# Attention and a SwiGLU block on one core: splitting 448 keys as three chunks of 128 and a rest of 64 that four heads share

## The chip, the cores and the metric

The kernel runs on one core of a Trainium2 chip. The metric is the device time in microseconds (us). Before the change it is 453.3 us, the median of three runs (453.28 to 453.46). The profiled execution has a span of 451.7 us from its first to its last instruction.

A core has TensorE (matrix products; in the profile PE, and PEld for the load of its stationary operand), ScalarE (ACT), VectorE (DVE), GpSimd (POOL) and SyncE (SP), which here only issues transfers. TensorE writes into PSUM, which has eight banks of 512 float32 columns by 128 partitions. ScalarE and VectorE move results from there to SBUF.

## The reference, cut to what matters

Eight sequences of 448 tokens, twelve heads of 64: 96 softmax attentions. Their outputs, joined to 768 features a token, go through a gated feed-forward block.

```python
batch, n_heads, seq, head_dim = (8, 12, 448, 64)
scores = scale * np.matmul(q, k.transpose(0, 1, 3, 2))
attn = np.exp(scores - np.max(scores, axis=-1, keepdims=True))
attn = attn / (np.sum(attn, axis=-1, keepdims=True) + 1e-09)
x = np.matmul(attn, v)                     # then (3584 tokens, 768)

n_tokens, d_model, d_ff = (3584, 768, 1536)
g = x @ w_gate
silu = g * (1.0 / (1.0 + np.exp(-g)))
out = silu * (x @ w_val) @ w_out
```

## The kernel before

Two heads of one sequence form a pair; there are 48. For a pair, `q` and `k` are turned so that the 64 features lie on partitions: head 0 on partitions 0 to 63, head 1 on 64 to 127. Pairs 0 to 10 are turned by TensorE, later ones by DMA transposes. The scores come with the keys on partitions, in four chunks of 112 keys. Both heads' matmuls contract 64 rows, each in its own half of the array, and one exponential on ScalarE takes both.

```python
P = 112; NC = S // P          # 4 chunks of 112 keys
NPE = 11; FIRST = 6; XPE = 12; NE = 4; NX = 6

def qk(pr, c):
    t = qkT[pr]
    s = ps_s.tile([128, 2, 512], FP32, tag="s")          # two banks, three such buffers
    for hx in range(2):
        nc.tensor.matmul(
            s[:, hx, 0:S],
            lhsT=t[ts(hx, 64), c * P : c * P + 128],
            rhs=t[ts(hx, 64), ds(S + (1 - hx) * D, S)],
            start=True, stop=True,
        )
    e = Es[pr % NE][:, ds(c * EB, 16)].rearrange("p (h b) x -> p h (b x)", h=2)
    nc.scalar.activation(e[:, :, 0:S], s[0:P, :, 0:S], AF.Exp, scale=sm_scale)
```

The product with the values has the queries on partitions. `vo` holds a column of ones after the 64 values, so that column 64 of the accumulator is the softmax sum. The 2 x 448 queries of a pair are seven blocks of 128, the last of which is half of each head; they share one bank. Four chunks times eight matmuls are 32 a pair. VectorE then divides.

```python
def pv_chunk(pr, c):
    if c == 0:
        accs[pr] = ps_f.tile([128, 512], FP32, tag="f", name="acc")   # one bank, two buffers
    ...
    for j in range(3):
        for hx in range(2):
            nc.tensor.matmul(a7[:, 2 * j + hx], lhsT=e[...128 queries], rhs=vo[:, hx, c, 0 : D + 1], ...)
    for hx in range(2):
        nc.tensor.matmul(a7[:, 6], lhsT=e[...64 queries and zeros], rhs=vo[:, hx, c, 0 : D + 1], ...)
    if c < NC - 1:
        return
    nc.vector.reciprocal(r[:, 0:7], a7[:, :, D])
    nc.vector.tensor_tensor(xt[:, 0:n], a7[:, 0:n, 0:D], r[...broadcast], ALU.mult)
    # ... pairs from XPE on: two small multiplications more, for the seventh block
```

`turn_x` turns the result so that features lie on partitions (X): pairs 0 to 11 by TensorE against an identity (with `turn_rests` for the seventh blocks of six pairs together), later ones by DMA transposes. X feeds the feed-forward block, which is cut into eight blocks of 384 or 512 tokens. A step `fv` makes 128 hidden features of a block: six matmuls for the gate (`gp`), six for the value (`vp`), a tanh on ScalarE (`sg`), two operations on VectorE (`t`, `hts`). A step `o` makes 128 tokens by 384 output features with twelve matmuls (`op`), which ScalarE evicts and SyncE stores.

```python
gp = ps_s.tile(...)[:, 0]            # or one of the two small banks, after a visit without a product
group("g", gp)                       # 6 matmuls of 128 x n
nc.scalar.activation(sg[:, 0:n], gp[:, 0:n], AF.Tanh, scale=0.5)
vp = ps_f.tile([128, 512], FP32, tag="f", name="vp")
group("v", vp)
...
last = last_block and ch == n // 128 - 1      # the last 128 tokens: stored in three parts
```

The program first does the attention of pairs 0 to 5 (one whole sequence), then goes through *visits*. A visit makes the next two or three score chunks, the product of a pair whose exponentials are ready, and the steps `fv` and `o` of an earlier sequence. After the last pair only feed-forward steps remain.

Of the kernel before, what the change touches and what calls it, by code (L numbers as in the profile page):

```python
# [19 lines left out]
NPE = 11  # L20
# [3 lines left out]
WIDE = 8  # L24
XPE = 12
NE = 4
NX = 6
NV = 5
VS = 9
EB = 15  # L30
# [3 lines left out]
def kernel(  # L34
# [24 lines left out]
    MQ = S - D  # L59
# [13 lines left out]
    load_table("exp_and_others")  # L73

# [7 lines left out]
    ps_f = ctx.enter_context(tc.tile_pool(name="ps_f", bufs=2, space=PSUM))  # L82

    Es = [consts.tile([P, NC * EB + 1, D], FP16, name=f"E{i}") for i in range(NE)]
    Xts = [consts.tile([128, 7, D], FP16, name=f"xt{i}") for i in range(NX)]
    Xrs = [consts.tile([D, 128], FP16, name=f"xr{i}") for i in range(3)]
    Vts = [consts.tile([P, 2, NC, D + 2], FP16, name=f"vo{i}") for i in range(NV)]
    vraw = consts.tile([P, VS, 2, NC, D], FP16, name="vraw")
# [11 lines left out]
    wo = [consts.tile([128, NFB, OH], FP16, name=f"wo{i}") for i in range(2)]  # L100
# [5 lines left out]
    def dummy(n):  # L106
        wp = ps_f.tile([128, 512], FP32, tag="f", name="wp")
        for _ in range(n):
            nc.tensor.matmul(wp[:], lhsT=warm[:, 0:128], rhs=warm[:], start=True, stop=True)  # L109

    def load_qk32(pr):
        rq = raws.tile([P, 2, NC, D], FP32, tag="rq", bufs=RB)
        rk = raws.tile([P, 2, NC, D], FP32, tag="rk", bufs=RB)
        for dst, src in ((rq, q), (rk, k)):
            nc.sync.dma_start(dst[:], src[0, 2 * pr : 2 * pr + 2].rearrange("h (p c) d -> p h (c d)", c=NC))
        raw[pr] = (rq[:], rk[:])
# [3 lines left out]
    def load_qk16(pr, n=2):  # L120
        h0 = 2 * (pr % 2) if pr >= 14 else 0
        if h0 == 0:
            q16 = raws.tile([P, 4, NC, D], FP16, tag="rq", bufs=RB, name="q16")
            k16 = raws.tile([P, 4, NC, D], FP16, tag="rk", bufs=RB, name="k16")
            pairbuf[:] = [q16, k16]
        q16, k16 = pairbuf
        for dst, src in ((q16, q), (k16, k)):
            flat = src.rearrange("b h s d -> (b h) s d")[2 * pr : 2 * pr + 2 * n]
            nc.gpsimd.dma_start(dst[:, ds(h0, 2 * n)], flat.rearrange("h (p c) d -> p h (c d)", c=NC))  # L129
        for i in range(n):  # L130
            h = h0 + 2 * i
            raw[pr + i] = (q16[:, h : h + 2], k16[:, h : h + 2])

    def load_v(pr, n=1):
        b, h = divmod(2 * pr, H)
        nc.gpsimd.dma_start(  # L136
            vraw[:, ds(pr % VS, n)].rearrange("p r h c d -> p (r h) (c d)"),
            v[b, h : h + 2 * n].rearrange("h (p c) d -> p h (c d)", c=NC),
        )
# [4 lines left out]
    def load_w(kind, i):  # L144
        if kind == "o":
            src = moe_w_out[:, ts(i, OH)].rearrange("(f p) m -> p f m", p=128)
            dst = wo[i]
        else:
            src = (moe_w_gate if kind == "g" else moe_w_val)[:, ts(i, DF // 4)].rearrange(
                "(t a p) m -> t p a m", p=128, t=2  # L150
            )
            for t in range(2):
                nc.gpsimd.dma_start(wgv[kind, i][:, ts(t, NCB // 2), :], src[t])
            return
        nc.gpsimd.dma_start(dst[:], src)

    def prep(pr):
        rq, rk = raw[pr]
        if pr == 0 or pr >= NPE:
            qk16 = attp.tile([P, 2, NC, 2, D], FP16, tag="qk16", bufs=3)  # L160
            for t, src in enumerate((rq, rk)):
                dst = qk16[:, 1 - t].rearrange("p c h d -> p h c d")
                if pr == 0:
                    nc.vector.tensor_copy(dst[:, 0], src[:, 0])
                    nc.scalar.activation(dst[:, 1], src[:, 1], AF.Copy)
                else:
                    nc.gpsimd.tensor_copy(dst, src)  # L167
        qkT[pr] = attp.tile([128, 2 * S + D], FP16, tag="qkT", name="qkT", bufs=5)
        if pr >= NPE:
            nc.sync.dma_start_transpose(  # L170
                qkT[pr][:, 0 : 2 * S].rearrange("p (c q) -> p c q", q=P),
                qk16[:].rearrange("p t c h d -> p (t c h d)"),
            )
            nc.sync.dma_start_transpose(
                qkT[pr][:, 2 * S :].rearrange("p (c q) -> p c q", c=1),
                qk16[0:D, 1, 0].rearrange("p h d -> p (h d)"),
            )
            return None

        def turn0():  # L180
            for t in range(2):
                tp = ps_s.tile([128, 2, 512], FP32, tag="s", name="tp")
                for c in range(NC):
                    for hx in range(2):
                        nc.tensor.matmul(
                            tp[ts(hx, 64), c // 2, ds(c % 2 * P, P)],
                            lhsT=qk16[:, 1 - t, c, hx],
                            rhs=ident[0:P, 0:P],
                            start=True,
                            stop=True,  # L190
                        )
                dst = qkT[pr][:, ts(1 - t, S)].rearrange("p (a x) -> p a x", a=2)
                nc.vector.tensor_copy(dst[:, 0], tp[:, 0, 0 : 2 * P])
                nc.scalar.activation(dst[:, 1], tp[:, 1, 0 : 2 * P], AF.Copy)
                if t == 0:
                    tq = tp
            nc.vector.tensor_copy(qkT[pr][:, 2 * S :], tq[:, 0, 0:D])

        def turn():
            if pr < FIRST + 2:  # L200
                tp = ps_s.tile([128, 2, 1024], FP16, tag="s", name="tp")[:, 0]
            else:
                tp = ps_f.tile([128, 1024], FP16, tag="f", name="tp")
            for i in range(2 * NC + 1):
                t, c = (1 - i // NC, i % NC) if i < 2 * NC else (0, 0)
                for hx in range(2):
                    src = raw[pr][t][:, hx, c, :]
                    nc.tensor.transpose(tp[ts(hx, 64), ts(i, P)], src, ident[0:P, 0:P])  # L208
            nc.vector.tensor_copy(qkT[pr][:], tp[:, 0 : 2 * S + D])  # L209

        return turn if pr else turn0

    def qk(pr, c):
        t = qkT[pr]
        s = ps_s.tile([128, 2, 512], FP32, tag="s")
        for hx in range(2):
            nc.tensor.matmul(  # L217
                s[:, hx, 0:S],
                lhsT=t[ts(hx, 64), c * P : c * P + 128],
                rhs=t[ts(hx, 64), ds(S + (1 - hx) * D, S)],  # L220
                start=True,
                stop=True,
            )
        e = Es[pr % NE][:, ds(c * EB, 16)].rearrange("p (h b) x -> p h (b x)", h=2)
        nc.scalar.activation(e[:, :, 0:S], s[0:P, :, 0:S], AF.Exp, scale=sm_scale)  # L225

    def qk_half(pr, half, between=None):
        for c in (2 * half, 2 * half + 1):
            qk(pr, c)
            if between and c % 2 == 0:  # L230
                between()
# [3 lines left out]
    def pv_chunk(pr, c):  # L235
        if c == 0:
            accs[pr] = ps_f.tile([128, 512], FP32, tag="f", name="acc")
        e = Es[pr % NE]
        vo = Vts[pr % NV]
        a7 = accs[pr][:, 0 : 7 * (D + 1)].rearrange("p (s d) -> p s d", s=7)  # L240
        for j in range(3):
            for hx in range(2):
                nc.tensor.matmul(  # L243
                    a7[:, 2 * j + hx],
                    lhsT=e[:, ds(c * EB + 9 * hx + 2 * j, 2)].rearrange("p b x -> p (b x)"),
                    rhs=vo[:, hx, c, 0 : D + 1],
                    start=c + j + hx == 0,
                    stop=False,
                )
        for hx in range(2):  # L250
            nc.tensor.matmul(  # L251
                a7[:, 6],
                lhsT=e[:, ds(c * EB + 6 + hx, 2)].rearrange("p b x -> p (b x)"),
                rhs=vo[:, hx, c, 0 : D + 1],
                start=False,
                stop=c == NC - 1 and hx == 1,
            )
        if c < NC - 1:
            return
        r = attp.tile([128, 8], FP32, tag="R", bufs=2, name="R")  # L260
        xt = Xts[pr % NX]
        nc.vector.reciprocal(r[:, 0:7], a7[:, :, D])  # L262
        n = 7 if pr < XPE else 6
        nc.vector.tensor_tensor(  # L264
            xt[:, 0:n],
            a7[:, 0:n, 0:D],
            r[:, 0:n].unsqueeze(2).to_broadcast([128, n, D]),
            ALU.mult,
# [373 lines left out]
```

The softmax here doesn't subtract the row's maximum and nothing guards it: scores larger than these inputs give would overflow.

## Time and profile before

| What | Value |
|---|---|
| Device time, median of 3 | 453.3 us |
| Span of the profile | 451.7 us |
| Exponentials, ScalarE | 192, of 919 ns |
| Score matmuls, 64 rows by 448 columns | 384 |
| Product matmuls, 112 rows by 65 columns | 1536 |
| Gate, value and output matmuls | 576, 576, 684 |
| Turns of q and k by DMA, turns of X by DMA | 37 pairs, 36 pairs |
| Loads of q, k and v that GpSimd issues, one issue | 660 to 666 ns |

How to read it: a row of the profile names a source line, an engine and an operation, then out<-in by tile names, partitions by elements, and the count. `s` are scores, `E` exponentials, `acc` a product's accumulator, `xt` the divided result, `tp` a turn in PSUM. The duration of a matmul in the profile includes its latency and overlaps with the next one; the distance between starts says how often the array takes one. The profile's share of busy time is a mean over stages that have different limits.

### The profile page before, as it was taken

Reading aid. Unit: us, or ns where it says so; the run is one execution under the profiler, and the core shown is the slowest. Engines: PE = TensorE matmul, PEld = TensorE weight load, DVE = VectorE, ACT = ScalarE, POOL = GpSimd, SP = SyncE. Lnnn points to the kernel's source line nnn. Section 1 sums busy time; section 2 is a strip of 40 time slices with the busy share of each in tenths; the row PEclk is TensorE's granted clock in tenths of the full one; section 3 lists DMA queues with packets and bytes.
Section 4 is the critical chain, followed back from the end, with each engine's and each line's share of the span. In section 5 each row is a group of like instructions: output and inputs, shape, how many; then the busy total and the mean of one; then the engine's idle time right before and its main releaser. Section 6 shows DMA issues by size and latency. Waiting matters only on the chain.

```text
span 451.7 us, 9871 instructions
## 1 busy us (share of the span) xinstructions
PE 441.9 (98%) x4024; PEld 247.0 (55%) x4024; DVE 201.6 (45%) x447; ACT 238.8 (53%) x350; POOL 141.8 (31%) x228
## 2 busy tenths in 40 slices
PE   8999999999999999999999999999999999999995
PEld 3655565545455556454555656545455666544563
DVE  3666562456654434455443534353453544055300
ACT  6965666566746465554554546644555462222221
POOL 8755715927642225252313405330100000000000
PEclk9999999999999999999999999999999999999999
DMA  9999999999969379874749758772503112200033
GB/s 142 173 200 201 196 172 174 180 209 119 145 93 133 46 129 124 132 120 71 126 74 120 98 78 143 118 105 68 101 20 68 46 46 57 70 2 0 17 100 95
DMA packets 105101, 48.71 MB, mean 108 GB/s; under 512 B 59744, under 2 KB 101600, under 8 KB 105056
## 3 DMA queue, kind: packets, MB, share of 16 engines
q0 software_dynamic: 43392, 23.37, 41.2%
q1 hardware_dynamic: 61664, 24.71, 28.9%
q8 instruction: 31, 0.51, 0.5%
q14 instruction: 14, 0.11, 0.1%
HBM read 47.19 MB, written 11.01 MB: 129 GB/s over the span
## 4 chain that ended last, share of the span: by engine, by line
PE 93%; DVE 3%; ACT 2%; issue 1%; DVEq 0%; ACTq 0%
PE op L371 24%; PE gp L326 23%; PE vp L326 23%; PE s L217 9%; PE acc L243 9%; PE acc L251 2%; ACT E L225 2%; PE tp L208 1%; PE wp L109 1%; DVE t L345 1%; ACT sg L341 1%; DVE qkT L209 0%; DVE xt L264 0%; PE acc L291 0%; DVE hts L348 0%
## 5 line engine op out<-in xcount | busy, mean ns | idle before, releaser
L225 ACT ACTIVATE E<-s 112x896 f16<-112x896 f32 x192 | 162.1, 919 | 27.5 <-PE s L217 27.4
L326 PE MATMUL gp<-X,wg 128*128 128x384 f16 (+1 forms) x576 | 124.7, 352 | 0.0
L326 PE MATMUL vp<-X,wv 128*128 128x384 f16 (+1 forms) x576 | 124.6, 352 | 0.0
L371 PE MATMUL op<-wo,hts 128*128 128x384 f16 (+1 forms) x684 | 116.1, 323 | 0.0
L345 DVE SCALAR_TENSOR_TENSOR t<-sg,gp 128x384 f32<-128x384 f32 (+1 forms) x96 | 59.7, 621 | 121.8 <-ACT sg L341 121.8
L341 ACT ACTIVATE sg<-gp 128x384 f32<-128x384 f32 (+1 forms) x96 | 52.5, 547 | 84.8 <-PE gp L326 83.6
L371 PEld LDWEIGHTS <-hts 128*128 128x128 f16 x684 | 65.5, 98 | 45.9 <-issue 3.9
L326 PEld LDWEIGHTS <-wv 128*128 128x128 f16 x576 | 56.3, 98 | 52.6
L326 PEld LDWEIGHTS <-wg 128*128 128x128 f16 x576 | 53.1, 97 | 45.6 <-issue 1.1
L378 ACT ACTIVATE osb<-op 128x384 f32<-128x384 f32 (+1 forms) x57 | 27.8, 487 | 92.5 <-PE op L371 92.5
L167 POOL COPY qk<-q 112x512 f16<-112x512 f16 x37 | 22.9, 619 | 144.5 <-DMA qkT<-qk 143.1
L348 DVE SCALAR_TENSOR_TENSOR hts<-t,vp 128x384 f16<-128x384 f32 (+1 forms) x96 | 59.6, 621 | 10.0
L243 PEld LDWEIGHTS <-E 112*128 112x128 f16 x1152 | 46.7, 97 | 18.2 <-issue 17.5
L243 PE MATMUL acc<-vo,E 112*128 112x65 f16 x1152 | 53.0, 193 | 1.3 <-DVE vo L142 0.7
L217 PE MATMUL s<-qkT 64*128 64x448 f16 x384 | 50.6, 355 | 0.2
L251 PE MATMUL acc<-vo,E 112*128 112x65 f16 x384 | 42.9, 193 | 0.0
L262 DVE RECIPROCAL R<-acc 128x7 f32<-128x7 f32 x48 | 9.8, 205 | 70.6 <-PE acc L251 70.5
L129 POOL DMA_DIRECT2D k<-in_k_dram x44 | 29.0, 660 | 9.5 <-DMA wo<-in_moe_w_out_dram 7.8
L129 POOL DMA_DIRECT2D q<-in_q_dram x44 | 29.3, 666 | 5.2 <-PE s L217 2.5
L136 POOL DMA_DIRECT2D vraw<-in_v_dram x42 | 28.0, 666 | 8.4 <-DVE vo L142 7.2
L217 PEld LDWEIGHTS <-qkT 64*128 64x128 f16 x384 | 14.5, 94 | 25.8 <-issue 18.6
L264 DVE TENSOR_TENSOR xt<-acc,R 128x384 f16<-128x384 f32 (+1 forms) x48 | 27.6, 574 | 1.7
(41 smaller groups left out, 148.2 us busy)
## 6 DMA issues: line engine op xcount, KB each, us to landing
q<-in_q_dram POOLq DMA_DIRECT2D x41, 112.0 KB, 4.0
k<-in_k_dram POOLq DMA_DIRECT2D x41, 112.0 KB, 4.6
vraw<-in_v_dram POOLq DMA_DIRECT2D x39, 112.0 KB, 4.6
wg<-in_moe_w_gate_dram POOLq DMA_DIRECT2D x8, 288.0 KB, 10.1
wv<-in_moe_w_val_dram POOLq DMA_DIRECT2D x8, 288.0 KB, 10.2
wo<-in_moe_w_out_dram POOLq DMA_DIRECT2D x2, 1152.0 KB, 22.0
out_dram<-osb SPq DMA_DIRECT2D x8, 288.0 KB, 3.0
out_dram<-osb SPq DMA_DIRECT2D x8, 240.0 KB, 3.1
```

The lines of the kernel that those rows point to most:

```text
L129: nc.gpsimd.dma_start(dst[:, ds(h0, 2 * n)], flat.rearrange("h (p c) d -> p h (c d)", c=NC))
L136: nc.gpsimd.dma_start(vraw[:, ds(pr % VS, n)].rearrange("p r h c d -> p (r h) (c d)"), v[b, h : h + 2 * n].rearrange("h (p c) d -> p h (c ...
L217: nc.tensor.matmul(s[:, hx, 0:S], lhsT=t[ts(hx, 64), c * P : c * P + 128], rhs=t[ts(hx, 64), ds(S + (1 - hx) * D, S)], start=True, stop=True,)
L225: nc.scalar.activation(e[:, :, 0:S], s[0:P, :, 0:S], AF.Exp, scale=sm_scale)
L243: nc.tensor.matmul(a7[:, 2 * j + hx], lhsT=e[:, ds(c * EB + 9 * hx + 2 * j, 2)].rearrange("p b x -> p (b x)"), rhs=vo[:, hx, c, 0 : D + 1] ...
L251: nc.tensor.matmul(a7[:, 6], lhsT=e[:, ds(c * EB + 6 + hx, 2)].rearrange("p b x -> p (b x)"), rhs=vo[:, hx, c, 0 : D + 1], start=False, st ...
L326: nc.tensor.matmul(dst[:, 0:n], lhsT=wslice(kind, fb, cb), rhs=X[kk][:, cb, ds(c0, n)], start=(cb == 0), stop=(cb == NCB - 1),)
L341: nc.scalar.activation(sg[:, 0:n], gp[:, 0:n], AF.Tanh, scale=0.5)
L345: nc.vector.scalar_tensor_tensor(t1[:, 0:n], sg[:, 0:n], 1.0, gp[:, 0:n], ALU.add, ALU.mult)
L348: nc.vector.scalar_tensor_tensor(hts[:, fb, 0:n], t1[:, 0:n], 0.5 * HS, vp[:, 0:n], ALU.mult, ALU.mult)
L371: nc.tensor.matmul(op[:, 0:w], lhsT=hts[:, fb, ts(ch, 128)], rhs=wo[oh][:, fb, ds(m0 - oh * OH, w)], start=(fb == 0), stop=(fb == NFB - 1),)
L378: nc.scalar.activation(osb[:, ds(m0, w)], op[:, 0:w], AF.Copy, scale=1.0 / HS)
```

## The change

The keys of a head are split otherwise: three chunks of 128 and a rest of 64. Head `hx` of pair `pr` has its rest at the front of its keys if `hx == pr % 2` ("low"), and at the back if not. So the rests of the four heads of two neighbouring pairs fill a whole 128-partition score tile of two banks: four 64x64 matmuls, one in each quadrant of the array, and one exponential. This is for filling all 128 partitions in the exponentials and in the main score and product matmuls. K and V are loaded so that keys lie 64 to a partition group, with the two halves of the partitions starting three key columns apart.

Further parts:
- TensorE turns q and k of pairs 0 to 13 (before 0 to 10), and X of pairs 0 to 17 (before 0 to 11). The rest of 64 queries is turned with the pair; `turn_rests` goes.
- A pair's product has an accumulator for each head: in the first six pairs and the last two one two-bank tile, between them the two small banks. In a visit, the X of the pair before is turned between the products of the two heads, into a score buffer.
- The six first pairs go by a fixed string of steps (`START`: s scores, t turn, v copy of values, p product piece, x turn of X, d idle matmul).
- The number of `fv` and `o` steps of each visit is planned ahead. The output steps of the first block run later, and `w_out` is loaded later, in four pieces.
- The first pair's q is loaded from ScalarE's queue and its k from SyncE's.
- In the output step a variable `n` is set to 112 inside the loop that stores rows.

```diff
-NPE = 11
+NPE = 14
-XPE = 12
+XPE = 18
-NX = 6
+NX = 3
+NR = 3
...
     def qk(pr, c):
-        t = qkT[pr]
         s = ps_s.tile([128, 2, 512], FP32, tag="s")
-        for hx in range(2):
-            nc.tensor.matmul(
-                s[:, hx, 0:S],
-                lhsT=t[ts(hx, 64), c * P : c * P + 128],
...
+        if c < KR:
+            t = qkT[pr]
             for hx in range(2):
                 nc.tensor.matmul(
+                    s[:, hx, 0:S],
+                    lhsT=t[ts(hx, 64), ts(c + low(pr, hx), 128)],
+                    rhs=t[ts(hx, 64), ds(NC * 128, S)],
...
+        else:
+            for hx in range(2):
+                for p in (pr, pr + 1):
+                    lo = low(p, hx)
+                    t = qkT[p]
+                    nc.tensor.matmul(
+                        s[ts(1 - lo, 64), hx, 0:S],
+                        lhsT=t[ts(hx, 64), ds(0 if lo else KR * 128 + 64, 64)],
+                        rhs=t[ts(hx, 64), ds(NC * 128, S)],
...
+            e = Ers[pr // 2 % NR][:]
...
+    def pv_mm(pr, hx, c, j):
+        lo = low(pr, hx)
...
+        if c < KR:
+            rows, e, col = slice(0, 128), Es[pr % NE][:, c], c + lo
+        else:
+            rows, e, col = (slice(0, 64), Ers[pr // 2 % NR], 0) if lo else (slice(64, 128), Ers[pr // 2 % NR], KR)
+        nc.tensor.matmul(
+            accs[pr][0][hx][:, ts(j, D + 1)],
+            lhsT=e[rows, ds(hx * S + j * 128, 128)],
+            rhs=Vts[pr % NV][rows, hx, col, 0 : D + 1],
...
+    def pv_open(pr):
+            if wide(pr):
+                acc = psum["a"].tile([128, 2, 512], FP32, tag="a", name="acc") if pr < FIRST else ps_s.tile(...)
+            else:
+                accs[pr] = ([fbank(), fbank()], [0, 0])
...
+    def pv(pr, mid):
+        for hx in range(2):
+            for c in range(KR):
+                pv_piece(pr, c, (hx,))
+            if hx == 0:
+                mid()                      # run_turns: turn_x of the pair before
+        pv_close(pr)
...
         if pr < XPE:
-            tp = accs[pr] if pr < FIRST else ps_f.tile([128, 512], FP32, tag="f", name="xtp")
-            for j in range(3):
+            tp = ps_s.tile([128, 2, 512], FP32, tag="s", name="xtp")[:, 0]
+            for j in range(KR + 1):
+                n = min(128, S - j * 128)
...
     def ffn2_steps(kk, c0, n, hts, first, last_block):
...
             last = last_block and ch == n // 128 - 1
...
-                    c, p0 = divmod((j + D) % S, P)
-                    m = min(P - p0, l0 + 128 - l, (MQ if j < MQ else S) - j)
+                    n = S // NC
+                    c, p0 = divmod(j, n)
+                    m = min(n - p0, l0 + 128 - l)
```

In a visit the shared rest's scores come first, then the chunks of 128, then the product's rest pieces, then its main pieces:

```diff
+                for pr, c in sorted(chunks, key=lambda x: -(x[1] == RU)):
+                    qk(pr, c)
+                for _, p0 in todo:
+                    pv_piece(p0, RU)
```

## The prediction

> **What bounds the kernel now.** I read the engine table of the page first, then the chain that ended last, then the stretches, and last the timeline of one cycle of the steady part.
>
> ```profile
> PE 441.9 (98%) x4024; PEld 247.0 (55%) x4024; DVE 201.6 (45%) x447; ACT 238.8 (53%) x350; POOL 141.8 (31%) x228
> ...
> PE 93%; DVE 3%; ACT 2%; issue 1%; DVEq 0%; ACTq 0%
> ```
>
> TensorE is on the chain for 93% of the span, so a microsecond taken from TensorE's own work is nearly a microsecond of time, and work taken from ScalarE (53%) or the DMA queues is not. The 98% alone would not prove that, since a pipelined matmul's duration holds its latency. So I looked where TensorE really waits (the stretches; columns: length, then busy time of PE, PEld, DVE, ACT and POOL):
>
> ```profile
> 6.00:30.00 24.00, 22.13 (x394) 14.23 (x394) 13.48 (x31) 22.10 (x27) 17.08 (x25) 1.00 1.33 178
> 30.00:86.00 56.00, 54.74 (x621) 33.68 (x620) 28.22 (x60) 34.42 (x49) 31.75 (x48) 1.00 1.34 182
> 86.00:386.00 300.00, 299.77 (x2657) 164.84 (x2654) 139.70 (x317) 164.90 (x243) 88.11 (x144) 1.00 0.65 101
> ```
>
> There are three regimes. Up to 29.8 us (the first `gp`) six pairs of heads go through attention before any feed-forward block can run; there TensorE and ScalarE are both over 90% busy. From 30 to 86 TensorE loses about 1.3 us. From 86 to 386 it loses nothing. After 386 there is only feed-forward, which the change hardly touches. So the costs of single instructions must come from the timeline (start, length, instructions):
>
> ```profile
> 207.21 2.11 PE L371 MATMUL op<-wo,hts 128*128 128x384 f16 x12
> 209.25 0.74 PE L217 MATMUL s<-qkT 64*128 64x448 f16 x6
> 209.93 0.36 PE L243 MATMUL acc<-vo,E 112*128 112x65 f16 x6
> ...
> 210.90 1.46 PE L326 MATMUL gp<-X,wg 128*128 128x512 f16 x6
> 212.20 1.46 PE L326 MATMUL vp<-X,wv 128*128 128x512 f16 x6
> 213.59 0.74 PE L217 MATMUL s<-qkT 64*128 64x448 f16 x6
> 214.26 1.96 PE L371 MATMUL op<-wo,hts 128*128 128x384 f16 x11
> ```
>
> Read start to start. Six 512-column matmuls take 212.20 - 210.90 = 1.30 us, 0.216 each, or 0.42 ns a column; 448 columns are then 0.19 us and 384 are 0.162. A product takes 210.90 - 209.93 = 0.97 us for its 32 matmuls: 0.030 each. Six score matmuls would be 1.13 us one by one, but the next group starts 0.68 us later: two run at once (three streams of 0.19), and about 0.1 us is left over. On the way in, six `vp` from 212.20 should end at 213.50, and the scores start at 213.59: again 0.1. So each change between 64-row scores and 128-row work costs 0.1 us.
>
> **What the Trainium skill says.** "TensorEngine Tiling (Array Packing)", Key Properties: a change of tiling mode drains the array, and different tiles run in parallel. Both agree with the trace (0.1 us; two scores in one stream). Its Available Configurations give four tiles in 64x64 mode; no trace here has four at once yet. "PSUM — Partial Sum Buffer", PSUM bank collisions, says that two row tiles may not write one bank at the same time, which fits the new code's separate bank for each head. "Perfetto Trace Analysis", Identifying the Most-Contended Engine, warns that matmul busy share is a bad measure, which is why I work from starts.
>
> **The change part by part, on TensorE.** Counts are from the order of the built instructions.
>
> 1. *Scores.* A head has 448 keys. Before, they were four chunks of 112; a pair cost four streams, 48 x 4 = 192 in all. Now each head has three chunks of 128 and a rest of 64, and the rests of two pairs (four heads) fill one 128-row score tile as four 64x64 matmuls. Streams: 48 x 3 + 24 = 168, if the four run together. 24 x 0.19 = **-4.5 us**. The exponentials fall from 192 to 168.
> 2. *Products.* Still 32 matmuls of 65 columns a pair, but 8 have only 64 keys, in opposite halves of the array for the two heads. If they run two by two, a pair of them should take about 0.033 us (64 columns in the trace's rest turns: 24 matmuls, 0.8 us busy with the latency of the last, hence some 0.03 per two). Before 32 x 0.0303 = 0.97; now 24 x 0.0303 + 4 x 0.033 = 0.86. 48 x 0.11 = **-5.3 us**.
> 3. *Turns of q and k.* TensorE turns pairs 0 to 13 now, not 0 to 10: three more. One turn was 18 matmuls in about 0.45 us (7.00 to 7.56 with a drain, in the first turn); the new one has 16 of 64 columns (0.24) and 8 of 112 (0.19). 14 x 0.43 against 11 x 0.43: **+1.4 us**, rounded up for the larger first two.
> 4. *Turns of X.* Eighteen pairs instead of twelve: 54 matmuls of 128 columns and 18 of 64, against 36 and 24 narrow ones. At 0.056 and 0.03: 3.5 against 2.4, **+1.1 us**.
> 5. *Mode changes.* Counting along TensorE's order, before has 172 and after 187. There are fewer visits (three score units each, fewer units), but a visit with a shared rest goes 128 -> 64x64 -> 64x128 -> 128, and a turn goes through 64x64 and 128x64. 15 x 0.1 = **+1.5 us**.
> 6. One idle matmul less: **-0.2 us**. Feed-forward is the same 774,144 columns; the last output piece is no longer split.
>
> Sum: -4.5 - 5.3 + 1.4 + 1.1 + 1.5 - 0.2 = **-6.0 us**.
>
> **Off TensorE.** *The start.* Its TensorE part falls by about 1.5 us (inside the sum), and ScalarE must do 21 exponentials, not 24, before the sixth pair's product: at 0.84 us each (6 in 5.04 us in the timeline) 2.5 us less. Against it, the accumulator of a pair is now a two-bank tile with one buffer, so each pair waits for the division of the one before; reciprocal and division took 0.2 and 0.63 us. I let the start gain just what TensorE's sum says. *The steady part.* A product now holds both small banks, so the last `vp` or `op` must be evicted before it. The scores and drains between take about 0.75 us; an `hts` of 512 columns takes 0.69 and an `osb` 0.49. It fits, barely. From 30 to 60 us VectorE has per visit about 3.9 us (two divisions, X, qkT, vo, t, hts, sized from their rows) against some 4.5 us of TensorE: tight, so I expect waits of about 2 us in all, as now. *The end.* In the new output step a loop variable `n` is overwritten with 112, so the test for the last piece is never true. The last 128 rows are then stored whole: an eviction of 0.49 instead of 0.33, then a 336 KB store behind a 48 KB one. The last split stores landed 2.0 us after issue, a large quiet one about 3.6, and the old end had four issues of 0.6 in a row, which go. Net **+0.8 us**.
>
> 453.3 - 6.0 + 0.8 = **448.1 us**.
>
> **Rivals.** *A: the small tiles don't run together.* For: four at once isn't seen in any trace here. Against: two by two is. Without it in the scores, +24 x 0.19 = 4.5 (452.6); without it in the products, +5.3 (453.4); with neither, 458. *B: PSUM becomes the wait.* Products now need both small banks, and each X turn takes a score buffer. For: the tight margins above. Against: VectorE is at 45%. At 0.1 us for some 50 visits, +5: 453. *C: the start was ScalarE's.* For: 22.10 busy of 24. Then the start falls by 2.5 or more, with q and k of the first pair on two queues: about 446.5. *D: GpSimd's issues.* Value and key loads come in two halves each: 224 loads instead of 148, and 76 more at 0.66 us are 50 us on an engine that is 31% busy. On the other side six turns of X and three of q and k leave the DMA transposes. I expect nothing of it after 90 us; in the first 90 us a late weight could cost 1 or 2 us.
>
> **Range and chances.** A and B push up by up to 5 us, C down by 2 and a perfect start by 3. I take 448.1 with 444.0 to 452.5. Faster by over 2% needs under 444.2, for which the start and every bank must work out: 0.11. Slower by over 2% (462.4) needs A twice and B: 0.02. Within 2%: 0.87.
>
> **What would show it.** Right: three score streams and a four-tile one of about 0.2 us start to start; 8 rest products in about 0.13 us; first `gp` at about 28 us; no TensorE waits over 0.3 us after 100 us; the last store landing about 1 us later after the last matmul than before. Wrong: rest products at 0.24 us a pair, `er` scores taking 0.38 or more (A); TensorE waiting for `f` evictions (B); TensorE waiting for a DMA (D); first `gp` after 30 us (the single accumulator).

## The result, and the profile after

The changed kernel takes 455.5 us, median of four runs (454.74 to 455.66), beside 453.38 us (453.28 to 453.64) for the kernel before on the same chip. The ratio is 1.0042, 95% interval 1.0025 to 1.006: 0.4% slower, and 3 us above the predicted range.

The engine table of the changed kernel's page, and the shares of its chain that ended last:

```profile
PE 441.6 (97%) x4163; PEld 248.8 (55%) x4163; DVE 206.0 (45%) x464; ACT 220.1 (48%) x325; POOL 178.8 (39%) x298
...
PE 79%; DMA 12%; POOL 3%; DVE 2%; ACT 2%; issue 1%; SPq 0%; DVEq 0%; POOLq 0%
```

TensorE's busy time is what it was (441.6 against 441.9), although it has less to do; the reason is that a matmul's duration contains its latency, so this figure can't show a saving. ScalarE lost 19 us, as 24 exponentials fell away. The new thing is the chain: 12% of it is now DMA, where there was none. The stretches (columns as in the prediction):

```profile
6.00:30.00 24.00, 22.71 (x451) 14.96 (x450) 14.92 (x32) 20.48 (x25) 17.56 (x27) 1.00 1.29 181
30.00:86.00 56.00, 52.60 (x701) 31.90 (x700) 35.96 (x84) 34.19 (x46) 36.01 (x57) 1.00 1.30 180
86.00:386.00 300.00, 298.62 (x2645) 166.92 (x2644) 134.63 (x307) 147.76 (x223) 120.42 (x204) 1.00 0.72 100
```

TensorE now stands still for 3.4 us between 30 and 86 (before 1.3) and 1.4 us after that (before 0.2). That is still too little, for the same reason: the latency of the last matmul hides the first part of every wait. So I went through the starts of all matmuls, and counted as a wait what a start comes later than the one before plus that one's own pace (0.19 us for 448 columns, 0.03 for 65, and so on) and the drain, where there is one. Between the first `gp` and 390 us this gives **9.4 us of waits** (5.85 before 90 us, 3.55 after), against 2.3 us in the kernel before. The span divides like this:

| Part of the span | Before, us | After, us | Difference |
|---|---|---|---|
| To the first `gp` | 29.79 | 28.07 | -1.7 |
| First `gp` to the end of the last matmul's columns | 416.6 | 420.6 | +4.0 |
| of which waits of TensorE | 2.3 | 9.4 | +7.1 |
| of which the rest, TensorE's own work | 414.3 | 411.2 | -3.1 |
| From there to the end | 5.34 | 5.16 | -0.2 |

The work did fall, and more waiting than that came in. Whose waits they are, in the changed kernel's list of waits, from 30 to 90 us (who waited <- for whom: us in total, times, longest):

```profile
PE tp L246 <- ACT er L277: 1.1, 2, 0.6
PE s L256 <- DMA qkT<-qk: 0.7, 1, 0.7
PE s L256 <- DVE X L371: 0.7, 1, 0.7
PE f L291 <- DVE hts L410: 0.5, 3, 0.2
```

and from 90 to 390 us:

```profile
PE f L291 <- DVE hts L410: 1.0, 5, 0.2
```

By my count from the starts, the last kind is the largest of all: 13 times a product's rest pieces wait for `hts` to give back the small bank, 0.18 to 0.36 us each and 3.9 us in all; the list shows 8 of them with what is left of each after the latency. The others are the score buffers (about 2.9 us until an exponential ends and a turn or a gate may write, 0.87 more for X's copy out of one), evictions of the output step (0.56) and one DMA transpose (0.88). The timeline of one visit of the changed kernel shows the bank wait (start, length, instructions):

```profile
212.68 1.46 PE L388 MATMUL f<-X,wv 128*128 128x512 f16 x6
214.07 0.74 PE L256 MATMUL s<-qkT 64*128 64x448 f16 x6
214.64 0.19 PE L291 MATMUL f<-vo,er 64*128 64x65 f16 x1
215.04 0.28 PE L291 MATMUL f<-vo,er 64*128 64x65 f16 x7 [0.20 <-DVE hts L410]
215.25 0.91 PE L291 MATMUL f<-vo,E 128*128 128x65 f16 x24
```

and VectorE in the same stretch:

```profile
214.30 0.69 DVE L410 SCALAR_TENSOR_TENSOR hts<-t,f 128x512 f16<-128x512 f32 x1
```

The value group ends at about 213.98 (212.68 and six times 0.216), the three pairs of scores take until 214.64. The first rest piece goes into one small bank; the second head's piece needs the other, from which VectorE is still multiplying (`hts` runs from 214.30 to 214.99), and starts at 215.04. The prediction knew this wait and called it a fit.

The same view has the good news. Another visit of the changed kernel, in which the bank was free:

```profile
238.33 0.38 PE L269 MATMUL s<-qkT 64*64 64x448 f16 x4
238.65 0.55 PE L256 MATMUL s<-qkT 64*128 64x448 f16 x4
239.03 0.28 PE L291 MATMUL f<-vo,er 64*128 64x65 f16 x8
239.25 0.91 PE L291 MATMUL f<-vo,E 128*128 128x65 f16 x24
239.99 0.81 PE L388 MATMUL gp<-X,wg 128*128 128x384 f16 x4
```

Four 64x64 scores take 238.65 - 238.33 = 0.32 us: one stream of 0.19 and a drain of some 0.12, so all four run together (their starts lie within 0.01 us). Eight rest pieces and the drain behind them take 0.22 us. The whole product takes 0.96 us from 239.03 to 239.99 with that drain inside it, against 0.97 before, where the drain lay ahead of it.

The chain leaves TensorE for the DMA at one place, 70.42 us; what it holds before that is almost all loads and GpSimd's issues of them. The chain of the changed kernel between 55 and 71 us (start, us, what):

```profile
55.93 0.75 POOL wo L173
...
57.59 0.78 POOL wo L173
58.36 1.18 POOL qk L195 x2
...
60.44 9.84 DMA qkT<-qk
70.42 0.37 PE s L256 x2
```

GpSimd issues two pieces of `w_out`, then copies pair 14's q and k for the transposes, of which the second takes 9.84 us to land, at 70.28; pair 14's first scores wait for it. Here that costs 0.88 us. But it is a second limit right behind the first: had TensorE come to 69 us earlier, it would have waited longer.

**Theories to test.** T1: the small banks (a product needs both at once) hold the steady part. T2: the DMA transpose of pair 14, behind `w_out` in a full queue, takes back whatever is gained before 70 us. Rival R1: the small tiles cost more than thought. Rival R2: moving X between the heads and turning pairs 12 to 17 on TensorE is what costs.

### The profile page after: what moved, and what is told of

Read it like the earlier page. It is cut to its first block, busy times and chain, and to the rows that moved or that the text cites. A ratio compares the mean times of both kernels' runs of the same rounds, so it can differ in the third digit from the quotient of the medians.

```text
span 453.9 us, 10198 instructions
## 1 busy us (share of the span) xinstructions
PE 441.6 (97%) x4163; PEld 248.8 (55%) x4163; DVE 206.0 (45%) x464; ACT 220.1 (48%) x325; POOL 178.8 (39%) x298
## 4 chain that ended last, share of the span: by engine, by line
PE 79%; DMA 12%; POOL 3%; DVE 2%; ACT 2%; issue 1%; SPq 0%; DVEq 0%; POOLq 0%
PE f L433 24%; PE f L388 22%; PE gp L388 20%; PE f L291 7%; DMA wv<-in_moe_w_val_dram 4%; PE s L256 4%; DMA wg<-in_moe_w_gate_dram 4%; DMA qkT<-qk 2%; DMA k<-in_k_dram 1%; PE s L269 1%; DVE hts L410 1%; DVE t L407 1%; ACT sg L403 1%; POOL vraw L124 1%; POOL q L154 0%
## 5 line engine op out<-in xcount | busy, mean ns | idle before, releaser
L277 ACT ACTIVATE E<-s 128x896 f16<-128x896 f32 x144 | 123.0, 922 | 12.9 <-PE s L256 12.6
L388 PE MATMUL f<-X,wv 128*128 128x384 f16 (+1 forms) x576 | 124.7, 353 | 0.0
L433 PE MATMUL f<-wo,hts 128*128 128x384 f16 x672 | 115.5, 326 | 0.0
L388 PE MATMUL gp<-X,wg 128*128 128x512 f16 (+1 forms) x522 | 113.4, 353 | 0.3
L440 ACT ACTIVATE osb<-f 128x384 f32<-128x384 f32 x56 | 27.5, 491 | 107.0 <-PE f L433 102.9
L410 DVE SCALAR_TENSOR_TENSOR hts<-t,f 128x384 f16<-128x384 f32 (+1 forms) x96 | 59.6, 621 | 10.1 <-PE f L388 0.2
L124 POOL DMA_DIRECT2D vraw<-in_v_dram x82 | 50.8, 645 | 5.8 <-DMA wv<-in_moe_w_val_dram 1.8
L291 PEld LDWEIGHTS <-E 128*128 128x128 f16 x1152 | 38.5, 97 | 3.9 <-issue 1.4
L291 PE MATMUL f<-vo,E 128*128 128x65 f16 x960 | 37.8, 193 | 0.0
L337 DVE TENSOR_TENSOR xt<-f,R 128x256 f16<-128x256 f32 x80 | 34.0, 425 | 2.8
```

The costliest lines, as they stand in the source:

```text
L124: eng.dma_start(dst[ts(s, 64)], rows)
L277: nc.scalar.activation(e[:, 0 : 2 * S].rearrange("p (h q) -> p h q", h=2), s[:, :, 0:S], AF.Exp, scale=sm_scale)
L291: nc.tensor.matmul(accs[pr][0][hx][:, ts(j, D + 1)], lhsT=e[rows, ds(hx * S + j * 128, 128)], rhs=Vts[pr % NV][rows, hx, col, 0 : D + 1], ...
L337: nc.vector.tensor_tensor(xt[:, :, hx], a4[:, :, 0:D], r[:].unsqueeze(2).to_broadcast([128, KR + 1, D]), ALU.mult,)
L388: nc.tensor.matmul(dst[:, 0:n], lhsT=wslice(kind, fb, cb), rhs=X[kk][:, cb, ds(c0, n)], start=(cb == 0), stop=(cb == NCB - 1),)
L410: nc.vector.scalar_tensor_tensor(hts[:, fb, 0:n], t1[:, 0:n], 0.5 * HS, vp[:, 0:n], ALU.mult, ALU.mult)
```

## The experiments

All were compared with runs of the kernel before on the same chip. To set a kernel beside the changed one I take the difference of the two ratios times 453.4 us; each ratio has an interval of about +-0.002, or 1 us, so a difference between two kernels is uncertain by 1 to 1.5 us. Waits are those of a run's one profiled execution.

**e1: pairs 12 and 13 turned by DMA.** `NPE = 14` becomes `NPE = 12`.

> The changed kernel with pairs 12 and 13 turned by DMA again (NPE 12). My theory (TensorE's own work fell as worked out, and waits for PSUM buffers ate it): two turns less, 2 x (0.43 us of matmuls + 3 drains of 0.1) = 1.5 us off TensorE, and the 0.12 us waits behind them; the product's waits stay. 453.8 us, from 455.5. Rival (the turns on TensorE are what spared the DMA queue): the transposes of pair 12 land late and TensorE waits for qkT by more than the 0.9 us that it waits for pair 14 now: 456 or more.

Measured 457.84 us, ratio 1.0082 (1.0061 to 1.0104), 1.8 us slower than the changed kernel. My own expectation fell. In its list of waits:

```profile
PE s L256 <- DMA qkT<-qk: 4.0, 2, 2.7
```

By starts 4.36 us, where it was 0.88. With these turns on DMA, TensorE waits for the transposes of pair 12 (until 59.2 us) and longer than before for those of pair 14 (until 72.1). Turning pairs 12 and 13 on TensorE is worth its cost.

**e2: X of pairs 12 to 17 turned by DMA.** `XPE = 18` becomes `XPE = 12`.

> The changed kernel with X of pairs 12 to 17 turned by DMA (XPE 12). My theory: six X turns of 0.2 us less on TensorE and no score buffer taken by them, so the waits of 0.16 to 0.28 us between 117 and 127 us go too: 453.4 us. The product's waits for the second small bank stay as they are. Rival (DMA turns of X hold up the next block): TensorE waits for X by DMA at the start of a block, 455.5 or more.

Measured 453.37 us, ratio 0.9986 (0.9956 to 1.0017): 2.5 us faster than the changed kernel, and level with the kernel before. The waits fall from 9.4 to 7.5 us, and TensorE's own work behind the first `gp` by 1.2 us, which is what six turns of about 0.2 us make (three matmuls of 0.056 and one of 0.03). This part of the change costs more than it brings.

**e3: X turned at the end of the visit, not between the heads.**

```diff
-                pv(p0, run_turns)
+                pv(p0, lambda: None)
...
+            run_turns()        # after the visit's steps
```

> The changed kernel with X turned at the end of the visit, not between the heads of the next product. My theory: TensorE's work is the same; the turn no longer takes the first free score buffer in the middle of a product, so the gate after it need not wait for the second exponential (about 1.5 us of such waits in the trace): 454.3 us. Rival (the place between the heads hides VectorE's division): waits for xt and for X in the early visits grow, 456.5 or more.

Measured 458.03 us, ratio 1.0084 (1.0066 to 1.0102), 1.9 us slower than the changed kernel. Its waits:

```profile
PE s L256 <- DVE X L371: 6.8, 11, 0.8
```

By starts 12 waits and 8.9 us. X's score buffer is then asked for by the third score piece, too soon. So the place between the heads is right, and with e2 R2 is half right: the place helps, six more pairs don't.

**e4: the small bank given back early.** A probe: the multiplication that makes `hts` reads `vp` for 64 of its columns only, and for the others multiplies `t` by `t`, so that `vp` is left out there.

```diff
-                hts[:, fb, 0:n], t1[:, 0:n], 0.5 * HS, vp[:, 0:n], ALU.mult, ALU.mult
+                hts[:, fb, 0:64], t1[:, 0:64], 0.5 * HS, vp[:, 0:64], ALU.mult, ALU.mult
+            # and a second multiplication
+                hts[:, fb, 64:n], t1[:, 64:n], 0.5 * HS, t1[:, 64:n], ALU.mult, ALU.mult
```

> A probe, not the reference's result: the last multiplication of a feed-forward step reads the value bank for 64 columns only, and the other columns multiply t by itself, so that VectorE's work stays and the small bank comes free some 0.5 us earlier. My theory (a product waits for its second small bank until hts has read it): the waits on hts between 34 and 320 us, about 4 us in all, go nearly wholly: 451.7 us. Rival (drains and tile modes, or the score buffers, cost the time): within 0.5 us of 455.5.

Measured 454.4 us, ratio 1.0011 (0.9985 to 1.0036): 1.4 us faster, no more than the uncertainty, and not the 3.9 us of waits that it takes away. Those waits did go (3.9 to 0.4). But in the profiled execution, the slowest of its six at 456.91, the waits for a score buffer until an exponential ends rose from 2.9 to 4.9 us, and the wait for pair 14's transpose from 0.88 to 2.7. T1 is half the story: the score buffer comes free only just after the small bank.

**e5: the rest pieces head by head.**

```diff
+        if c == RU:
+            for hx in heads:
+                for j in range(KR + 1):
+                    pv_mm(pr, hx, c, j)
+            return
```

> The changed kernel with a product's rest pieces in the order of the heads (four of head 0, then four of head 1) instead of alternating. My theory (alternating 64-row matmuls run two by two, so the prediction's -5.3 us for the products is real and was eaten by waits): TensorE has 48 x 4 x 0.030 = 5.8 us more to do, less the 1 us or so that it waits there anyway: 460 us. Rival (the pairs never ran together, the gain was never there): within 1 us of 455.5.

Measured 457.55 us, ratio 1.0087 (1.0064 to 1.0111): +2.0 us, about half of the expected loss. One visit of it:

```profile
230.50 0.74 PE L256 MATMUL s<-qkT 64*128 64x448 f16 x6
231.08 0.34 PE L291 MATMUL f<-vo,er 64*128 64x65 f16 x8
```

The eight starts lie within 0.156 us (0.096 when the heads alternate), not the 0.21 of eight in a row at 0.03 each. As the starts go (0, 0.029, 0.064, 0.068, 0.093 and on), the second head's matmuls, in the other half of the array, begin about 0.065 us after the first head's and run beside them. That is 0.06 us a product more, 2.9 us in 48; of the waits, those for `hts` fall from 3.9 to 2.7 us and the one for pair 14's transpose rises from 0.88 to 2.5, so the +2.0 us is not the order of the pieces alone. Alternating is still right, and R1 falls: the small tiles do what they were made for.

**b1: another order in visits without a product.** There the output step goes last, the gate takes the small bank first, the turn of q and k comes behind the `fv` steps, and X is turned only in the next product.

```diff
-            if x + 7 < NPE:
+            if x + 7 < NPE and not (bare and x):
                 prep(x + 7)()
...
-                if bare and no:
-                    run_o()
-                    no -= 1
...
-                    if bare and y == 0:
-                        run_turns()
+                if x + 7 < NPE and bare and x:
+                    prep(x + 7)()
                 for _ in range(no):
                     run_o()
```

> The changed kernel with another order in the visits without a product: feed-forward step first (gate in a small bank), then the turn of q and k, output step last, and X turned in the next product. Same work. My theory (waits for buffers ate the gain): the two waits of 0.6 us of a turn for a score buffer, the one of 0.9 us for X, and four of 0.36 us after such visits go: 455.5 - 3.3 = 452.2 us. Rival (something else than buffer waits): no change over 0.5 us.

Measured 459.74 us, ratio 1.0153 (1.0128 to 1.0179). Its waits:

```profile
PE f L433 <- DVE t L407: 4.8, 5, 1.1
```

The expectation fell: an output step behind a single `fv` needs the gate's small bank, and waits for VectorE's `t` five times. The scores wait twice more for the copy of a turn (2.6 us by starts). Order within a visit is an order of requests for the two banks, and I had looked at one request only.

**b2: b1, with the rest pieces after the main ones where the visit before ended with a value group.**

```diff
-                    pv_piece(p0, RU)
+                    if not ended_v[0]:
+                        pv_piece(p0, RU)
...
-                pv(p0, run_turns)
+                pv(p0, run_turns, ended_v[0])    # the rest pieces last
```

> b1 with the product's rest pieces behind its main pieces in visits that follow a value group, so that the second small bank is needed some 0.5 us later. It costs one mode change of 0.1 us in each of some nine visits and takes away some nine waits of 0.18 to 0.36 us. My theory: 1.5 us less than b1, 450.7 us. Rival, after the bank probe: the wait only moves on to the score buffers, as much as b1.

Measured 460.21 us, ratio 1.017 (1.0142 to 1.0197). The waits for `hts` are gone; the X turns behind the product wait 2.6 us for score buffers instead.

**b3: b2 with `XPE = 12`.**

> b2 with X of pairs 12 to 17 turned by DMA. As that edit alone took 2.1 us from the changed kernel, of which some 1.2 us were TensorE's work: 449 us if my theory holds and the parts add; 451 if b2's parts have already taken its waits away.

Measured 456.42 us, ratio 1.0068 (1.0055 to 1.008): better than b2 by 4.6 us and still slower than the kernel before, since b1's waits for `t` and for the copy of a turn stay (8.2 us by starts).

**p1 and p2: both buffers taken away, in the changed kernel and in the one before.** Probes: e4's edit, and from pair 8 on the exponentials take 64 of 448 queries, so that score buffers come free early (most weights of those pairs are stale). This also takes work from ScalarE (34.19 to 16.62 us busy between 30 and 86 us), so the probe doesn't tell a late buffer from a slow ScalarE.

```diff
+        w = S if pr < FIRST + 2 else 64
...
-            ... s[:, :, 0:S], AF.Exp, scale=sm_scale
+            ... s[:, :, 0:w], AF.Exp, scale=sm_scale
```

> A probe, not the reference's result: the changed kernel with the value bank read for 64 columns only (as in the bank probe) and, from the ninth pair on, exponentials of 64 of the 448 queries, so that score buffers and small banks come free early; TensorE's instructions are the same. My theory (TensorE's own work fell as predicted, waits for buffers ate it): some 7 of the 9.4 us of waits behind the first gate go: 448 us, the predicted time. Rival (the work itself is not smaller): no nearer to the freed kernel of before than now. A wait for qkT of pair 14 by DMA may stay or grow, as TensorE gets there earlier.

> The same probe on the kernel of before, as the other side of the comparison. It waits only 2.3 us behind its first gate, so my theory expects little: 452 us, and 4 to 5 us more than the freed changed kernel. Rival (exponentials are on the path of both kernels): both fall by the same.

Measured: p1 454.18 us, ratio 1.0012 (0.9999 to 1.0025); p2 452.39 us, 0.9983 (0.9965 to 1.0001). With nearly every buffer wait gone (0.56 us left after 90 us), the changed kernel is still not faster than the kernel before. The timeline of p1 tells why:

```profile
65.79 0.55 PE L256 MATMUL s<-qkT 64*128 64x448 f16 x4
70.83 0.56 PE L256 MATMUL s<-qkT 64*128 64x448 f16 x2 [4.49 <-DVE vo L168]
...
73.22 2.11 PE L389 MATMUL gp<-X,wg 128*128 128x384 f16 x6
75.12 1.53 PE L389 MATMUL f<-X,wv 128*128 128x384 f16 x6
```

TensorE reached pair 14 at 66 us and stood for 4.65 us. The profile names a copy of values, which these scores don't read. It is only the last event: that copy waited for a value load which took 8.3 us to land. Pair 14's transposes, issued at 58.8 and 60.2, needed 9.9 and 10.5 us as well: the second landed at 70.69, 0.14 us before the scores, as in the changed kernel (70.28 and 70.42). Both are DMA. What TensorE had gained, it gave back here, and more: for some 5 us after the wait its matmuls ran at half rate (the six `gp` take 1.90 us, 0.317 each, where 384 columns take 0.162). T1 alone does not hold; whether T2 does is tested by f1 and f2.

**b4: the changed kernel with `XPE = 12` and the rest pieces last as in b2** (without b1's order).

> The changed kernel in its own order of steps, with two edits: X of pairs 12 to 17 turned by DMA, and the product's rest pieces last in visits that follow a value group. Alone the first gave 453.4. My theory: of the 4.2 us of waits on hts some 1.5 us remain as added mode changes and some move to the score buffers: 452 us. Rival (they all move on): 453.4.

Measured 452.45 us, ratio 0.9984 (0.9964 to 1.0004). The profiled execution, the slowest of its six at 455.28, waits 3.0 us for the transpose of pair 14.

**b5: b4, with the turn of q and k ahead of the scores in visits without a product, and X only between heads.**

```diff
+                if x + 7 < NPE and not todo:
+                    prep(x + 7)()
...
-                    if bare and y == 0:
-                        run_turns()
```

> b4 with the turn of q and k ahead of the scores in the two early visits without a product, and X turned only between the heads of a product. My theory: the two waits of 0.6 us for a score buffer shrink to about 0.25 each and the one of 0.9 us for X goes: 1.5 us less than b4, 450.5 us. Rival (the third score piece then waits for the copy of qkT, as in b1): b4's time or more.

Measured 452.51 us, ratio 0.9988 (0.9969 to 1.0006): no gain beside b4. Six executions lie from 451.86 to 454.57.

**f1: the changed kernel with `w_out` loaded later.**

```diff
-            9: [("o", 0), ("o", 1)],
-            11: [("o", 2), ("o", 3)],
+            13: [("o", 0)],
+            14: [("o", 1), ("o", 2)],
+            15: [("o", 3)],
```

> The changed kernel with the loads of w_out moved from the entry of pairs 9 and 11 to that of pairs 13 to 15, behind the DMA turns of pair 14. Theory now (two limits side by side: buffers, and the DMA queue that is full up to 70 us): only the wait of 0.9 us for qkT of pair 14 can go, the buffer waits stay: 454.6 us. Rival (buffers alone): 455.5. If w_out came too late, TensorE would wait for it near 100 us.

Measured 455.14 us, ratio 1.0035 (1.0016 to 1.0053): -0.3 us, less than its uncertainty. The wait for the transpose is gone, the buffer waits are all there (8.6 us). Pair 14's transposes are now issued at 56.4 and 57.7 us, 2.7 us earlier, since GpSimd does not issue `w_out` first, and land in 3.6 and 4.6 us, not in 9.1 and 9.8. So the late landing was `w_out`'s doing, by the order of issue and by the load on the queues; but alone, T2's cure does nothing for the time either.

**f2: p1 and f1 together** (a probe, with p1's omissions).

> A probe, not the reference's result: the freed changed kernel (short exponentials and early value bank) with w_out loaded later. Theory now: the wait of 4.7 us at 66 us and the 2 us of half rate behind it go, and nothing else stands in the way: 447.5 us, against 452.4 for the freed kernel of before. Rival (a third limit): 451 or more.

Measured 449.15 us, ratio 0.9903 (0.9878 to 0.9928): 6.3 us faster than the changed kernel. One of its six executions, at 455.08 us, fell in a slower state of the chip and is left out of the ratio; the median of the other five is 448.67. p1 took 1.4 us off, f1 0.3; together they take 6.3. Its stretch from 30 to 86 us:

```profile
30.00:86.00 56.00, 54.59 (x714) 33.13 (x713) 40.95 (x104) 18.15 (x48) 42.00 (x67) 1.00 1.31 168
```

and the same of p1:

```profile
30.00:86.00 56.00, 50.58 (x654) 31.05 (x652) 34.67 (x93) 16.62 (x43) 37.43 (x59) 0.94 1.35 181
```

4.0 us more work is done by 86 us, at the full clock (1.00, not 0.94). This is the decisive run. Beside p2, the kernel before with the same omissions, it is 3.6 us faster by the ratios (3.7 by the medians, 452.39 and 448.67), though it still waits 3.6 us in places; p2 keeps the old loading of `w_out`, and no transpose is waited for there.

**f3: the best order with nothing left out:** b5 with `w_out` later as in f1.

> b5 with w_out loaded later; nothing left out. Theory now: those runs of b5 that wait 3 us for pair 14 no longer do: 450.3 us. Rival: 452.5 as b5.

Measured 451.57 us, ratio 0.9964 (0.9944 to 0.9985): faster than both kernels. By starts it waits 4.4 us; the longest in its list is

```profile
PE f L435 <- DMA wo<-in_moe_w_out_dram: 0.9, 1, 0.9
```

`w_out` is now late itself, once.

**f4: f3, with the values of pair 1 loaded alone,** ahead of pair 4's q and k (`load_v(1, 2)` becomes `load_v(1)`, and `load_v(2)` follows later).

> f3 with the values of pair 1 loaded by themselves, ahead of those of pair 2. In b5's profile TensorE waited 1.2 us at 12.7 us for the values of pair 1 and then ran at half rate up to 18 us, so that the first gate came at 29.6 us instead of 27.3. Theory now: that late start goes where it comes up, 450 us or a little less. Rival: the other loads come later in turn, as f3.

Measured 452.79 us, ratio 0.999 (0.9969 to 1.0011). The expectation fell: it is 1.2 us slower than f3, inside the uncertainty, and in its profile a key load is now late (0.69 us of wait at 29.4 us).

**f5: f3, with `w_out` at pairs 13 and 14 and X behind the rest pieces in visits where these come last.**

> f3 with the last piece of w_out loaded with the third, at the entry of pair 14, and with X turned behind the rest pieces in the visits where these come last. Theory: the wait of 1.0 us for w_out near 100 us goes, and about 1.2 of the 1.6 us in which an X turn waits for a score buffer: 449.6 us. Rival: w_out collides with the DMA turns again (a wait near 68 us), or VectorE's copy of X holds up the division: 451.6 or more.

Measured 451.58 us, ratio 0.9959 (0.9945 to 0.9972): the same as f3. It waits 4.2 us, now three times at a value group, for VectorE's division of the product (1.0 us). The waits move once more instead of going.

## Why the prediction was wrong, step by step

- **Scores (1) and products (2): right in mechanism.** The four 64x64 scores cost one stream, and eight rest pieces take 0.22 us with their drain (predicted 0.13 + 0.1). Rival A, that they don't run together, fell.
- **Mode changes (5): a little too small.** A drain from 64x64 to 64x128 costs about 0.12 us (0.31 us start to start for a stream of 0.19), not 0.1. 24 visits at 0.02 us more are 0.5 us.
- **The sum of TensorE's work: -6.0 predicted.** The starts give -1.7 - 3.1 = -4.8 us. The two freed kernels, f2 and p2, differ by 3.6 us while f2 still has 3.6 us of waits by its starts and p2 1.0; that would be about -6.2. The work term was about right; where in -4.8 to -6.2 it lies stays open.
- **The start: right in direction, and its size by luck.** The first `gp` came 1.7 us earlier (predicted 1.5) in this execution. In the other runs, whose start is the same or nearly so, it came between 27.13 (f2) and 29.64 us (b5), that is 2.7 to 0.2 us earlier than before, so rival C's 2.5 is as much within it as the 1.5.
- **The end: wrong in sign, and small.** +0.8 predicted, -0.2 measured: the last 336 KB store landed 2.8 us after its issue, where the prediction took about 3.6, and the last landing comes 3.9 us after the last matmul in both kernels. The overwritten `n` was not tried by itself.
- **The step that failed: "It fits, barely ... I expect waits of about 2 us in all, as now."** Measured 9.4 us. The margin for the bank was worked out as scores and drains of 0.75 us against an `hts` of 0.69. The 0.69 is right. Two terms were wrong. `hts` doesn't start when the value group ends (213.98) but 0.32 us later, at 214.30; the prediction left that out. And the rest pieces come 0.66 us after that end, at 214.64, as there is no drain between 64-row scores and 64-row rest pieces. So the bank is due after 0.66 us and free after 0.32 + 0.69 = 1.01. A miss of some 0.3 us, 13 times, is 3.9 us. The score buffers, for which X turns and turns of q and k now ask beside scores and gates, add about 3.8 us in the same way and were left out of the sum. Rival B had this at +5 us (453) and was given too little weight. The Trainium skill's "Perfetto Trace Analysis", Optimization Strategy, says that the same gap, repeated on the engine that should be full, can mean too few buffers; the 13 waits of 0.18 to 0.36 us are such gaps.
- **The second failure: "in the first 90 us a late weight could cost 1 or 2 us".** It was not a weight but pair 14's transpose, and it was not a fixed cost. It is a time (70 us) before which pair 14 can't start. The prediction added gains as if nothing stood behind TensorE. p1 comes to the scores of that visit 3.4 us earlier than the changed kernel (65.79 against 69.15) and gets on with pair 14 0.4 us later (70.83 against 70.42).

So the difference of +2.1 us is -4.8 of work and start, -0.2 at the end and +7.1 of waits. Shown by runs: the buffers and the transpose each hide the other (p1, f1, f2); X of pairs 12 to 17 on TensorE costs 2.5 us (e2); pairs 12 and 13 on TensorE and the place between the heads each help by about 1.9 us (e1, e3). Not settled: which of f3's remaining 4.4 us could still go, since each order tried moved them.

## What to carry to other kernels

When TensorE is full, list for every PSUM buffer who asks for it next and how long before that its last reader ends; a margin of 0.06 us on paper that was missed by some 0.3 us in 13 visits took back 3.9 us. Two limits that lie close together hide each other: taking away one brought 0.3 or 1.4 us, little beside an uncertainty of 1 to 1.5, taking away both 6.3, so a cure that does nothing alone is not yet refuted. Before counting an early gain, look up when the next transfer lands and who needs it.

## What the runs showed of the hardware

Transposes by DMA landed in 2.4 to 7.5 us (median 3.8) between 120 and 380 us, where the DMA moved about 100 GB/s (the stretch from 86 to 386), and in 3.7 to 11.5 us (median 9.4) between 40 and 90 us, where it moved about 180 (30 to 86). With `w_out` loaded later (f1) the second median is 5.8.

After a wait TensorE can run at half rate. The Trainium skill's "TensorE: Matmul & The Clock Gate", What's actually happening, gives an idle window of about 3.4 us for it. p1's wait of 4.65 us agrees (stretches of p1, the granted clock is the third number from the end):

```profile
66.00:71.00 5.00, 0.51 (x6) 0.16 (x4) 1.30 (x3) 0.47 (x2) 2.96 (x5) 0.81 1.58 143
71.00:76.00 5.00, 5.00 (x47) 3.33 (x44) 1.76 (x6) 0.77 (x2) 5.00 (x10) 0.51 1.43 185
```

It was 1.00 again from 76 to 80 us.

But in b5 a wait of only 1.24 us, which began behind the scores of 12.74 us, was enough (stretches of b5):

```profile
12.00:14.00 2.00, 1.00 (x8) 0.51 (x9) 0.86 (x3) 1.98 (x3) 0.74 (x2) 1.00 1.30 175
14.00:16.00 2.00, 1.83 (x38) 1.53 (x37) 0.84 (x3) 0.97 (x2) 1.99 (x3) 0.67 1.40 190
16.00:18.00 2.00, 2.00 (x33) 1.22 (x33) 1.34 (x3) 0.92 (x1) 2.00 (x4) 0.50 1.37 189
```

So in that execution a missed transfer in the start cost its wait and again some 1.7 us (2 us at 0.67 and 2 us at 0.50). In e5 a wait of 2.5 us, until 71.54, was followed by the full clock (1.00 from 71 to 78 us). So the length of one wait alone does not decide it; what does, no run here settles. And matmuls that use different row halves need not alternate in program order to overlap: the starts of eight in head order lie within 0.156 us (e5), where one by one they would span 0.21.
